# A decode block's MLP tail: w_out in longer runs, z2 before z1, three moving columns for w_out, and 1/std last

## The chip, the cores and the metric

The kernel runs on one core of a Trainium2 chip. The time is device microseconds from the first to the last instruction of that core, as a median over runs. A profile is one execution, recorded instruction by instruction. Engines are named as in the profile: PE (matmuls), PEld (their weight loads), DVE (vector), ACT (scalar), POOL (GpSimd), SP (the engine that issues nearly all transfers).

## The reference

A decode step for four sequences (B = 4, one new position each, model width D = 512), conditioned by c:

```python
mod = silu(c) @ w_mod                       # six vectors sa, ca, ga, sb, cb, gb of width 512
h = layernorm(x) * (1 + ca) + sa
x = x + ga * attention(h, k_cache, v_cache, wq, wo)   # 32 heads of 128, 4096 cached positions
h = layernorm(x) * (1 + cb) + sb
z = gelu(h @ w_in)                          # width 1792, halves z1 and z2 of 896
g = w_sp * layernorm(z2) + b_sp             # w_sp and b_sp are single numbers here (S = 1)
x = x + gb * ((z1 * g) @ w_out)
```

All inputs are bf16. The two caches hold 4 x 32 x 4096 x 128 values each, 134 MB; they make up most of the bytes.

Since the layer norm of z2 is (z2 - m) * r with one m and one r (1/std) per sequence, the last line splits: with a = (z1 * z2) @ w_out and b = z1 @ w_out, the result is gb * (w * r * a + (bs - w * r * m) * b). So w_out can be multiplied before m and r are known.

## The kernel before, in words

Everything is laid out feature-major: width 512 is four column blocks j of 128 partitions, width 896 is seven blocks jf (JF = 7), and the four sequences are the moving columns of each matmul. A vector such as modT[:, 5] (gb) is 128 partitions x 4 blocks x 4 sequences, 16 numbers per partition.

The stages are these. A preamble (lines 221 to 263) computes silu(c), LN1, the modulation (mod_part) and the queries. mod_part reads w_mod as weights: for its first two calls the 128 columns have a step of 4 elements, for the other four they are contiguous. The preamble also prepares gwb (line 258): gb times w_sp and gb times b_sp. Then a loop over 32 pairs of a head group and a sequence (lines 417 to 449) streams K and V in tiles of 4 MB and does the attention of each; two K and two V buffers alternate. SP issues the transfers in program order. In the last round it issues, after the last V pieces, the last tile of wo (line 427), the two halves of w_in (win, line 429) and the two parts of w_out (wout, line 431). The trace's names for these tiles are wo_g, win_434, win_435, wout_436 and wout_437.

The part after the loop (lines 457 to 519) is one serial tail, whose engines run their instructions in the order written:

- x1 (lines 460, 461), LN2 and h (lines 464 to 472). ln_stats forms squares, sums over the partitions with a matmul against a matrix of equal entries, reduces, and takes 1/std on ACT as Ln and then Exp.
- z (line 480): 56 matmuls. The outer loop is over the halves a of w_in. On half 0 all blocks of z2 (s = 1) and z1 (s = 0) get their first two terms, on half 1 their last two.
- gelu of z2 (line 487) and of z1 (line 491), an ACT table load back to the set that has Ln and Exp (line 492), and LN3's sums over z2 with the product z1 * z2 in between (line 494). u holds the product and z1 side by side, so that w_out has eight moving columns.
- y (line 499): 28 matmuls, first those on wout_436, then those on wout_437.
- six vector operations after Exp: gb*w*r (line 505), times m (506), gb*bs minus that (507), times y (508), the sum of the two (510), plus x1 (512). Then a transpose by matmul (514), a copy (518) and the store (519).

w_out's rows are taken as seven blocks of 128: partition p holds rows p, 128 + p, 256 + p and so on, each 1 KB long, so that one run in memory is one row.

Of the kernel before, what the change touches and what calls it, by code (L numbers as in the profile page):

```python
# [8 lines left out]
BF16 = mybir.dt.bfloat16  # L9
F32 = mybir.dt.float32  # L10
AF = mybir.ActivationFunctionType
ALU = mybir.AluOpType
# [4 lines left out]
def kernel(  # L17
# [16 lines left out]
    nc = tc.nc  # L34
    ctx.enter_context(tc.manual_schedule())
    P = 128
    B, _, D = A_x.shape
    _, H, SK, DH = A_k_cache.shape
    F = B_w_in.shape[1]
    FH = F // 2  # L40
    J = D // P
    JF = FH // P
# [12 lines left out]
    persist = ctx.enter_context(tc.tile_pool(name="persist", bufs=1))  # L55
# [40 lines left out]
    def load_k(i):  # L96
        return load(A_k_cache, i, "kt", (2, 2) if i == len(quads) - 1 else (1,))

    def load_v(i):
        return load(A_v_cache, i, "vt", (2, 4, 8, 16, 16) if i == len(quads) - 1 else (1,))  # L100
# [13 lines left out]
        out=sel, in_=ident.rearrange("p (t m) -> p m t", m=32), axis=AX.X, op=ALU.add,  # L114
# [33 lines left out]
    def bc(col, n):  # L148
        return col[:, None, :].to_broadcast([P, n, B])
# [25 lines left out]
    modT = persist.tile([P, 6, J, B], F32, name="modT")  # L175
    qbc = persist.tile([P, B, G, DH], BF16, name="qbc")
    x1b = persist.tile([P, 2, J, B], F32, name="x1b")
    wbf = persist.tile([P, 2], F32, name="wbf")
# [1 line left out]
    cT, x4T = xcT[:, :, 0:B], xcT[:, :, B:2 * B]  # L180
    xT = persist.tile([P, J, B], F32, name="xT")

    gwb = persist.tile([P, 2, J, B], F32, name="gwb")
    sT = persist.tile([P, J, B], BF16, name="sT")
    hbc = persist.tile([P, J, B, R], BF16, name="hbc")
    psum_acc = ctx.enter_context(
# [34 lines left out]
    with tc.tile_pool(name="pre", bufs=1) as pre:  # L221
        xc_ps = psum_s.tile([P, J, 2 * B], F32, name="small", bufs=1)
        for j in range(J):
            nc.tensor.matmul(
                xc_ps[:, j, :], lhsT=rows[:, j::J],
                rhs=ident[0:2 * B, 0:2 * B], start=True, stop=True,
            )
        xt_ps = psum_s.tile([P, J, B], F32, name="big", bufs=2)
        for j in range(J):
            nc.tensor.matmul(  # L230
                xt_ps[:, j, :], lhsT=rows[:, j * P:(j + 1) * P],
                rhs=ident[0:2 * B, B:2 * B], start=True, stop=True,
            )
        xb = pre.tile([P, 2, J, B], F32, name="xb")
        sg = pre.tile([P, J, B], F32, name="sg")
        nc.scalar.activation(out=sg, in_=xc_ps[:, :, 0:B], func=AF.Exp, scale=-1.0)
        nc.vector.tensor_copy(out=xcT, in_=xc_ps)
        nc.vector.tensor_copy(out=xb[:, 0], in_=x4T)
        nc.vector.tensor_scalar_add(out=sg, in0=sg, scalar1=1.0)
        nc.vector.reciprocal(out=sg, in_=sg)  # L240
        nc.vector.tensor_tensor(out=sT, in0=sg, in1=cT, op=ALU.mult)
        mean, rstd = ln_stats(pre, psum_s, xb, mean_d, J, "ln1")
        nc.vector.tensor_copy(out=xT, in_=xt_ps)
        mod_part(1)
        mod_part(0)
        hn = pre.tile([P, J, B], F32, name="hn")
        nc.vector.tensor_tensor(out=hn, in0=xb[:, 0], in1=bc(mean, J), op=ALU.subtract)
        nc.vector.tensor_tensor(out=hn, in0=hn, in1=bc(rstd, J), op=ALU.mult)
        nc.vector.tensor_tensor(out=hn, in0=hn, in1=modT[:, 1], op=ALU.mult)
        nc.vector.tensor_tensor(out=hn, in0=hn, in1=modT[:, 0], op=ALU.add)  # L250
        nc.vector.tensor_copy(out=hbc, in_=hn[:, :, :, None].to_broadcast([P, J, B, R]))
        for oc in range(2, 6):
            mod_part(oc)
        wb_ps = psum_s.tile([P, 2], F32, name="small", bufs=1)
        nc.tensor.matmul(wb_ps, lhsT=ones_b, rhs=wb_t, start=True, stop=True)
        nc.vector.tensor_copy(out=wbf, in_=wb_ps)
        for k in range(2):
            nc.vector.tensor_scalar_mul(out=gwb[:, k], in0=modT[:, 5], scalar1=wbf[:, k:k + 1])
        for b in range(B):
            for g0 in range(0, G, 4):  # L260
                qp = psum_s.tile([P, 4, DH], F32, name="big", bufs=2)
                query(b, g0, 4, qp)
                nc.scalar.copy(out=qbc[:, b, g0:g0 + 4, :], in_=qp)


    with tc.tile_pool(name="psum_att", bufs=1, space=bass.MemoryType.PSUM) as psum:
# [112 lines left out]
        def apply(i):  # L379
# [28 lines left out]

        win_v = B_w_in.rearrange("(j p) n -> p j n", p=P)
        win = [persist.tile([P, 2, F], BF16, name=f"win{a}") for a in range(2)]  # L410
        JFS = [(0, JF // 2 + 1), (JF // 2 + 1, JF)]
        wout_v = B_w_out.rearrange("(j p) n -> p j n", p=P)
        wout = [
            persist.tile([P, j1 - j0, D], BF16, name=f"wout{a}") for a, (j0, j1) in enumerate(JFS)
        ]
        st["k", 0] = load_k(0)
        for i in range(NQ):
            if i + 1 < NQ:
                st["k", i + 1] = load_k(i + 1)
            if quads[i][1] == 0:  # L420
                g = quads[i][0]
                st["wo", g] = wk.tile([P, NH, D], BF16, name="wo_g", bufs=2)
                if g < G - 1:
                    nc.sync.dma_start(out=st["wo", g], in_=wo_w[g])
            st["v", i] = load_v(i)
            if i == NQ - 1:
                nc.sync.dma_start(out=st["wo", G - 1], in_=wo_v[G - 1])
                for a in range(2):
                    nc.sync.dma_start(out=win[a], in_=win_v[:, 2 * a:2 * a + 2, :])
                for a, (j0, j1) in enumerate(JFS):  # L430
                    nc.sync.dma_start(out=wout[a], in_=wout_v[:, j0:j1, :])
            if i > 1:
                diagonal(i - 2)
            if i == NQ - 1:
                keep_busy(4)
            scores(i, 0)
            if i > 1:
                project(i - 2)
            scores(i, 1)
            if i == NQ - 1:  # L440
                softmax(i - 1)
            fold(i, 0)
            fold(i, 1)
            if i != NQ - 2:
                softmax(i)
            if i > 0:
                values(i - 1)
            if i > 1:
                apply(i - 2)
# [7 lines left out]
    with tc.tile_pool(name="post", bufs=1) as post, \  # L457
            tc.tile_pool(name="psum_post", bufs=1, space=bass.MemoryType.PSUM) as psum:
        x1 = x1b[:, 0]
# [4 lines left out]
        mean, rstd = ln_stats(post, psum_s, x1b, mean_d, J, "ln2", lambda:  # L464
            nc.vector.tensor_tensor(out=xs, in0=x1, in1=modT[:, 4], op=ALU.mult))
        nc.scalar.preload_act_table_set("gelu_apprx_tanh_and_others")
        ms = post.tile([P, J, B], F32, name="ms")
# [3 lines left out]
        h = post.tile([P, J, B], BF16, name="h")  # L471
        nc.vector.tensor_tensor(out=h, in0=xs, in1=modT[:, 3], op=ALU.add)

        zp = {s: psum.tile([P, JF, B], F32, name=f"z{s}_ps") for s in (1, 0)}
        for a in range(2):
            for s in (1, 0):
                for jf in range(JF):
                    c0 = s * FH + jf * P
                    for j in range(2):
                        nc.tensor.matmul(  # L480
                            zp[s][:, jf], lhsT=win[a][:, j, c0:c0 + P], rhs=h[:, 2 * a + j],
                            start=(a == 0 and jf == 0 and j == 0), stop=(a == 1 and j == 1),
                            skip_group_check=True,
                        )
        z2b = post.tile([P, 2, JF, B], F32, name="z2b")
        z2 = z2b[:, 0]
        nc.scalar.activation(out=z2, in_=zp[1], func=AF.Gelu_apprx_tanh)


        u = post.tile([P, JF, 2, B], BF16, name="u")  # L490
        nc.scalar.activation(out=u[:, :, 1, :], in_=zp[0], func=AF.Gelu_apprx_tanh)
        nc.scalar.preload_act_table_set("natural_log_exp_and_others")  # L492
        mean, rstd = ln_stats(post, psum_s, z2b, mean_f, JF, "ln3", lambda:
            nc.vector.tensor_tensor(out=u[:, :, 0, :], in0=u[:, :, 1, :], in1=z2, op=ALU.mult))
        y_ps = psum.tile([P, J, 2, B], F32, name="y_ps")
        for a, (j0, j1) in enumerate(JFS):
            for jf in range(j0, j1):
                for jo in range(J):
                    nc.tensor.matmul(
                        y_ps[:, jo], lhsT=wout[a][:, jf - j0, jo * P:(jo + 1) * P], rhs=u[:, jf],  # L500
                        start=(jf == 0 and jo == 0), stop=(jf == JF - 1), skip_group_check=True,
                    )

        cf = post.tile([P, J, 2, B], F32, name="cf")
        nc.vector.tensor_tensor(out=cf[:, :, 0], in0=gwb[:, 0], in1=bc(rstd, J), op=ALU.mult)
        nc.vector.tensor_tensor(out=ms, in0=cf[:, :, 0], in1=bc(mean, J), op=ALU.mult)
        nc.vector.tensor_tensor(out=cf[:, :, 1], in0=gwb[:, 1], in1=ms, op=ALU.subtract)
        nc.vector.tensor_tensor(out=cf, in0=y_ps, in1=cf, op=ALU.mult)
        q = post.tile([P, J, B], F32, name="q")
        nc.vector.tensor_tensor(out=q, in0=cf[:, :, 0], in1=cf[:, :, 1], op=ALU.add)  # L510
        yo = post.tile([P, B, J], BF16, name="yo")
        nc.vector.tensor_tensor(out=yo.rearrange("p b j -> p j b"), in0=q, in1=x1, op=ALU.add)
        t_ps = psum_s.tile([J * B, P], F32, name="small", bufs=1)
        nc.tensor.matmul(
            t_ps, lhsT=yo.rearrange("p b j -> p (b j)"), rhs=ident, start=True, stop=True,
# [34 lines left out]
```

## Time and profile before

The median of three runs is 671.23 us (671.2 to 671.52). The profiled execution took 671.3 us; its recorded span is 669.5 us.

| | busy in the span |
|---|---|
| PE | 414.7 us (62%) |
| DVE | 403.1 us (60%) |
| ACT | 41.3 us (6%) |
| POOL | 4.4 us (1%) |
| transfers | 283.17 MB at a mean of 423 GB/s |

Busy shares are averages over the whole span, and nearly all of it is the loop over K and V. The tail, which is all that the change touches, takes the last 12 us. It is read from the timeline, where each row has a start, a duration, the engine and line, the operation, the tiles (output <- inputs), the shape, and in brackets the idle time before it with what ended it. The chain of work is another view: followed back from the last instruction, it names at each step what released it. The granted clock of PE is 0.50 of full speed through the tail.

### The profile page before, as it was taken

To read this page: it belongs to the slowest core of one execution; us is meant where nothing else is said; L and a number is where in the kernel's file an instruction comes from. 1 tells how busy PE (TensorE), PEld (TensorE's weight loads), DVE (VectorE), ACT (ScalarE), POOL (GpSimd) and SP (SyncE) were. 2 spreads that over 40 slices of the span, in tenths; PEclk is the share of its full clock that TensorE was granted. 3 is DMA by queue.
4 is the path that set the end of the run, shared out by engine and by line. 5 is a ranking of instruction groups with operands and counts; after the bars stand their busy time and mean duration, and the time that the engine had idled before them with its cause. 6 is when DMAs were issued, how large, how long until landed. Compare 5 with 4: busy or idle time off the path is not lost.

```text
span 669.5 us, 6935 instructions
## 1 busy us (share of the span) xinstructions
PE 414.7 (62%) x3024; PEld 204.2 (30%) x3024; DVE 403.1 (60%) x476; ACT 41.3 (6%) x115; POOL 4.4 (1%) x20
## 2 busy tenths in 40 slices
PE   2557777655577655666655576665556655556775
PEld 2223333222233222233222333222223322223334
DVE  2166677666556676546666555756655657655752
ACT  1200000000000000000000000000000000000002
POOL 2000000000000000000000000000000000000000
PEclk9977777668887667888667888766788766788895
DMA  9999999999999999999999999999999999999995
GB/s 376 437 431 429 428 431 434 429 430 430 433 426 433 432 432 430 427 434 430 433 425 434 428 433 432 428 435 429 430 429 436 425 434 430 433 430 433 430 405 203
DMA packets 13373, 283.17 MB, mean 423 GB/s; under 512 B 1432, under 2 KB 2848, under 8 KB 4640
## 3 DMA queue, kind: packets, MB, share of 16 engines
q1 hardware_dynamic: 13264, 282.73, 98.7%
q8 instruction: 23, 0.38, 0.2%
q14 instruction: 6, 0.05, 0.0%
q0 software_dynamic: 64, 0.00, 0.0%
q10 hardware_dynamic: 16, 0.01, 0.0%
HBM read 282.73 MB, written 0.00 MB: 422 GB/s over the span
## 4 chain that ended last, share of the span: by engine, by line
DMA 61%; PE 24%; DVE 12%; ACT 1%; issue 0%; SPq 0%; DVEq 0%
DMA kt<-in_A_k_cache_dram 58%; PE s_ps L278 24%; DVE kt L273 11%; DMA wo_g<-in_A_wo_dram 3%; SPq L92 0%; PE big L338 0%; PE z_ps L480 0%; DVE S L287 0%; ACT L492 0%; ACT E L308 0%; DVE P_0_105 L311 0%; DVE P_1_109 L311 0%; PE small L155 0%; PE attn_ps L398 0%; DVE nm L305 0%
## 5 line engine op out<-in xcount | busy, mean ns | idle before, releaser
L278 PE MATMUL s_ps<-kt,ident 128*128 128x512 bf16 x1024 | 294.1, 459 | 189.0 <-DVE kt L273 189.0
L273 DVE TENSOR_TENSOR kt<-kt,qbc 128x8192 bf16<-128x8192 bf16 x64 | 282.7, 4420 | 85.9 <-DMA kt<-in_A_k_cache_dram 85.9
L278 PEld LDWEIGHTS <-ident 128*128 128x128 bf16 x1024 | 116.5, 114 | 355.3 <-issue 229.0
L287 DVE TENSOR_REDUCE S<-s_ps 128x64 f32<-128x512 f32 x64 | 44.3, 692 | 124.8 <-PE s_ps L278 124.8
L351 PE MATMUL zo_ps<-sel,osb 128*128 128x4 f32 x248 | 33.6, 259 | 25.8 <-ACT osb L344 25.8
L308 ACT ACTIVATE E<-S,nm 128x128 f32<-128x128 f32 x32 | 12.8, 401 | 567.2 <-DVE nm L305 567.2
L351 PEld LDWEIGHTS zo_ps<-sel,osb 128*128 128x128 f32 x248 | 31.1, 197 | 37.2 <-ACT osb L344 37.2
L338 PE MATMUL big<-vt,P_0_105 128*32 128x512 bf16 x352 | 21.0, 380 | 1.5 <-DMA vt<-in_A_v_cache_dram 1.5
L338 PE MATMUL big<-vt,P_2_113 128*32 128x512 bf16 x320 | 19.1, 380 | 0.0
L338 PE MATMUL big<-vt,P_1_109 128*32 128x512 bf16 x320 | 19.1, 380 | 0.0
L344 ACT COPY osb<-big 128x512 f32<-128x512 f32 x31 | 17.5, 565 | 20.1 <-PE big L338 20.1
L311 DVE TENSOR_TENSOR P_1_109<-E,mask_99 128x512 bf16<-128x512 f32 x11 | 7.6, 693 | 6.8 <-ACT E L308 6.8
L311 DVE TENSOR_TENSOR P_0_105<-E,mask_99 128x512 bf16<-128x512 f32 x11 | 7.6, 693 | 6.7 <-ACT E L308 6.7
L214 PE MATMUL big<-vt,hbc 128*32 128x512 bf16 x128 | 8.5, 430 | 5.0 <-DMA vt<-in_A_wq_dram 5.0
L338 PEld LDWEIGHTS <-P_0_105 128*32 128x32 bf16 x352 | 8.4, 96 | 9.0 <-DMA vt<-in_A_v_cache_dram 1.6
L311 DVE TENSOR_TENSOR P_2_113<-E,mask_99 128x512 bf16<-128x512 f32 x10 | 6.9, 693 | 6.2 <-ACT E L308 6.2
L372 DVE RECIPROCAL rz<-zo_ps 128x4 f32<-128x4 f32 x31 | 5.5, 176 | 8.4 <-PE zo_ps L351 8.4
L398 PE MATMUL attn_ps<-oP,wo_g 128*128 128x4 bf16 x112 | 3.8, 164 | 10.6 <-DVE oP L395 10.6
L338 PEld LDWEIGHTS <-P_1_109 128*32 128x32 bf16 x320 | 7.7, 96 | 6.7
L338 PEld LDWEIGHTS <-P_2_113 128*32 128x32 bf16 x320 | 7.6, 96 | 6.7
L398 PEld LDWEIGHTS <-wo_g 128*128 128x128 bf16 x128 | 4.3, 97 | 11.1 <-issue 10.4
L305 DVE STREAM_TRANSPOSE nm<-hb 128x32 f32<-128x32 f32 x32 | 6.8, 211 | 1.1
(218 smaller groups left out, 129.0 us busy)
## 6 DMA issues: line engine op xcount, KB each, us to landing
kt<-in_A_k_cache_dram SPq DMA_DIRECT2D x31, 4096.0 KB, 26.0
vt<-in_A_v_cache_dram SPq DMA_DIRECT2D x31, 4096.0 KB, 33.9
vt<-in_A_wq_dram SPq DMA_DIRECT2D x1, 4096.0 KB, 20.4
wo_g<-in_A_wo_dram SPq DMA_DIRECT2D x8, 512.0 KB, 26.6
kt<-in_A_k_cache_dram SPq DMA_DIRECT2D x2, 2048.0 KB, 25.6
vt<-in_w_mod_dram SPq DMA_DIRECT2D x1, 3072.0 KB, 9.9
vt<-in_A_v_cache_dram SPq DMA_DIRECT2D x1, 2048.0 KB, 18.7
vt<-in_A_v_cache_dram SPq DMA_DIRECT2D x1, 1024.0 KB, 20.8
```

The lines of the kernel that those rows point to most:

```text
L214: nc.tensor.matmul(qp[hl * R:(hl + 1) * R, 0:n], lhsT=hbc[:, j, b, :], rhs=wv[:, g0:g0 + n, hl, :], start=(j == 0), stop=(j == J - 1), til ...
L273: nc.vector.tensor_tensor(out=kt, in0=kt, in1=q[:, None, :].to_broadcast([P, HT, DH]), op=ALU.mult,)
L278: nc.tensor.matmul(ps, lhsT=ident, rhs=kt[:, :, cc * DC:(cc + 1) * DC], start=(cc == 0), stop=(cc == DH // DC - 1),)
L287: nc.vector.tensor_reduce(out=st["S", i][:, half * HT:(half + 1) * HT], in_=st.pop(("s", i, half)), axis=AX.X, op=ALU.add,)
L305: nc.vector.transpose(out=nm, in_=hb)
L308: nc.scalar.activation(out=E, in_=S, func=AF.Exp, bias=nm[:, 0:1], scale=att_scale, accum_out=rs,)
L311: nc.vector.tensor_tensor(out=P4[:, 0:NT, :], in0=E[:, :, None].to_broadcast([P, NT, NH]), in1=mask4[:, None, :].to_broadcast([P, NT, NH]) ...
L338: nc.tensor.matmul(po[32 * t:32 * t + 32], lhsT=P4[:, n0:n0 + 8, :], rhs=st["v", i][:, n0:n0 + 4, :], start=(u == 0), stop=(u == NU - 1), ...
L344: nc.scalar.copy(out=osb, in_=po)
L351: nc.tensor.matmul(st["o", i], lhsT=osb[:, n, :], rhs=sel[:, NH * n:NH * n + NH], start=(n == 0), stop=(n == 3),)
L372: nc.vector.reciprocal(out=rz, in_=st.pop(("z", i)))
L398: nc.tensor.matmul(attn_ps[:, jo, :], lhsT=wo_g[:, hl, jo * P:(jo + 1) * P], rhs=oT[:, hl, :], start=(g == 0 and hl == 0 and jo == 0), sto ...
```

## The change

Five things change in the tail, and one buffer in the preamble.

- w_out's rows are distributed differently. Of the first 512 rows, partition p holds rows 4p to 4p + 3, one run of 4 KB; of the last 384 rows it holds 3p to 3p + 2, one run of 3 KB.
- To match, the blocks of z take columns with a step: 4 for the first four blocks, 3 for the last three. These are weight loads of win with strided columns.
- The order of z is changed: for z2 first, every block with all four terms, and then the same for z1. The third matmul in order is now on the second half of w_in.
- u gets a third column group, z1 once more (the gelu writes 56 numbers per partition instead of 28), so w_out has twelve moving columns: for a, and twice for b.
- gwb becomes one tile with three groups: gb*w, a slot for -gb*w*m, and gb*bs. After the mean is known the slot is filled, gwb is multiplied by y in one operation, the third group is added to x1 on POOL (r1), the first two are added on DVE (q), q is multiplied by r, and r1 is added. Of these only the last two need Exp's result.

```diff
-    gwb = persist.tile([P, 2, J, B], F32, name="gwb")
+    gwb = persist.tile([P, J, 3, B], F32, name="gwb")
...
-        JFS = [(0, JF // 2 + 1), (JF // 2 + 1, JF)]
-        wout_v = B_w_out.rearrange("(j p) n -> p j n", p=P)
+        JFS = [(0, 4), (4, JF)]
+        wout_v = [
+            B_w_out[j0 * P:j1 * P].rearrange("(p j) n -> p j n", p=P) for j0, j1 in JFS
+        ]
...
-        for a in range(2):
-            for s in (1, 0):
-                for jf in range(JF):
-                    c0 = s * FH + jf * P
-                    for j in range(2):
+        for s in (1, 0):
+            for j0, j1 in JFS:
+                for jf in range(j0, j1):
+                    c0 = s * FH + j0 * P + jf - j0
+                    cols = slice(c0, c0 + (P - 1) * (j1 - j0) + 1, j1 - j0)
+                    for j in range(J):
                         nc.tensor.matmul(
-                            zp[s][:, jf], lhsT=win[a][:, j, c0:c0 + P], rhs=h[:, 2 * a + j],
-                            start=(a == 0 and jf == 0 and j == 0), stop=(a == 1 and j == 1),
-                            skip_group_check=True,
+                            zp[s][:, jf], lhsT=win[j // 2][:, j % 2, cols], rhs=h[:, j],
+                            start=(j == 0), stop=(j == J - 1),
                         )
...
-        u = post.tile([P, JF, 2, B], BF16, name="u")
-        nc.scalar.activation(out=u[:, :, 1, :], in_=zp[0], func=AF.Gelu_apprx_tanh)
+        u = post.tile([P, JF, 3, B], BF16, name="u")
+        nc.scalar.activation(
+            out=u[:, :, 1:3, :], in_=zp[0][:, :, None, :].to_broadcast([P, JF, 2, B]),
+            func=AF.Gelu_apprx_tanh,
+        )
...
-        y_ps = psum.tile([P, J, 2, B], F32, name="y_ps")
+        y_ps = psum.tile([P, J, 3, B], F32, name="y_ps")
...
-        cf = post.tile([P, J, 2, B], F32, name="cf")
-        nc.vector.tensor_tensor(out=cf[:, :, 0], in0=gwb[:, 0], in1=bc(rstd, J), op=ALU.mult)
-        nc.vector.tensor_tensor(out=ms, in0=cf[:, :, 0], in1=bc(mean, J), op=ALU.mult)
-        nc.vector.tensor_tensor(out=cf[:, :, 1], in0=gwb[:, 1], in1=ms, op=ALU.subtract)
-        nc.vector.tensor_tensor(out=cf, in0=y_ps, in1=cf, op=ALU.mult)
+        nc.vector.scalar_tensor_tensor(
+            out=gwb[:, :, 1], in0=gwb[:, :, 0], scalar=-1.0, in1=bc(mean, J),
+            op0=ALU.mult, op1=ALU.mult,
+        )
+        nc.vector.tensor_tensor(out=gwb, in0=y_ps, in1=gwb, op=ALU.mult)
         q = post.tile([P, J, B], F32, name="q")
-        nc.vector.tensor_tensor(out=q, in0=cf[:, :, 0], in1=cf[:, :, 1], op=ALU.add)
+        r1 = post.tile([P, J, B], F32, name="r1")
+        nc.gpsimd.tensor_tensor(out=r1, in0=gwb[:, :, 2], in1=x1, op=ALU.add)
+        nc.vector.tensor_tensor(out=q, in0=gwb[:, :, 0], in1=gwb[:, :, 1], op=ALU.add)
+        nc.vector.tensor_tensor(out=q, in0=q, in1=bc(rstd, J), op=ALU.mult)
         yo = post.tile([P, B, J], BF16, name="yo")
-        nc.vector.tensor_tensor(out=yo.rearrange("p b j -> p j b"), in0=q, in1=x1, op=ALU.add)
+        nc.vector.tensor_tensor(out=yo.rearrange("p b j -> p j b"), in0=q, in1=r1, op=ALU.add)
```

More of the change, by code (lines that the diff above doesn't have):

```diff
@@ L257 @@
         for k in range(2):
-            nc.vector.tensor_scalar_mul(out=gwb[:, k], in0=modT[:, 5], scalar1=wbf[:, k:k + 1])
+            nc.vector.tensor_scalar_mul(
+                out=gwb[:, :, 2 * k], in0=modT[:, 5], scalar1=wbf[:, k:k + 1],
+            )
         for b in range(B):
@@ L430 @@
                 for a, (j0, j1) in enumerate(JFS):
-                    nc.sync.dma_start(out=wout[a], in_=wout_v[:, j0:j1, :])
+                    nc.sync.dma_start(out=wout[a], in_=wout_v[a])
             if i > 1:
@@ L502 @@
                     )
-        cf = post.tile([P, J, 2, B], F32, name="cf")
-        nc.vector.tensor_tensor(out=cf[:, :, 0], in0=gwb[:, 0], in1=bc(rstd, J), op=ALU.mult)
-        nc.vector.tensor_tensor(out=ms, in0=cf[:, :, 0], in1=bc(mean, J), op=ALU.mult)
-        nc.vector.tensor_tensor(out=cf[:, :, 1], in0=gwb[:, 1], in1=ms, op=ALU.subtract)
-        nc.vector.tensor_tensor(out=cf, in0=y_ps, in1=cf, op=ALU.mult)
+        nc.vector.scalar_tensor_tensor(
+            out=gwb[:, :, 1], in0=gwb[:, :, 0], scalar=-1.0, in1=bc(mean, J),
+            op0=ALU.mult, op1=ALU.mult,
+        )
+        nc.vector.tensor_tensor(out=gwb, in0=y_ps, in1=gwb, op=ALU.mult)
         q = post.tile([P, J, B], F32, name="q")
-        nc.vector.tensor_tensor(out=q, in0=cf[:, :, 0], in1=cf[:, :, 1], op=ALU.add)
+        r1 = post.tile([P, J, B], F32, name="r1")
+        nc.gpsimd.tensor_tensor(out=r1, in0=gwb[:, :, 2], in1=x1, op=ALU.add)
+        nc.vector.tensor_tensor(out=q, in0=gwb[:, :, 0], in1=gwb[:, :, 1], op=ALU.add)
+        nc.vector.tensor_tensor(out=q, in0=q, in1=bc(rstd, J), op=ALU.mult)
         yo = post.tile([P, B, J], BF16, name="yo")
-        nc.vector.tensor_tensor(out=yo.rearrange("p b j -> p j b"), in0=q, in1=x1, op=ALU.add)
+        nc.vector.tensor_tensor(out=yo.rearrange("p b j -> p j b"), in0=q, in1=r1, op=ALU.add)
         t_ps = psum_s.tile([J * B, P], F32, name="small", bufs=1)
```

## The prediction

> **What bounds the kernel now.** I read the page first: the slices, the chain by line, the DMA issues. Then the chain of work in order of time for the last 15 us, the timeline of the same stretch, the instructions on w_out's second tile, and the matmuls of line 200, the only ones before the attention that load 128 weight columns with a stride. From the page:
>
> ```profile
> DMA  9999999999999999999999999999999999999995
> DMA 61%; PE 24%; DVE 12%; ACT 1%; issue 0%; SPq 0%; DVEq 0%
> ```
>
> The transfers are busy in every slice but the last; 283 MB at 423 GB/s fill the span. Nothing in the diff touches this stream before its last four issues (two halves of w_in, two of w_out). So the change can act only after the last wo tile has landed. The end of the chain, in order of time (start us, us, what):
>
> ```profile
> 634.51 23.00 DMA wo_g<-in_A_wo_dram
> ...
> 657.56 0.60 PE attn_ps L398 x16
> ...
> 660.90 0.18 DVE h L472
> 661.08 0.14 issue
> 661.22 1.78 PE z_ps L480 x56
> 663.00 0.02 issue
> 663.02 0.19 ACT u L491
> 663.21 0.02 issue
> 663.23 1.28 ACT L492
> 664.52 0.01 issue
> 664.53 0.31 ACT rstd_ln_4194 L170
> 664.83 0.02 issue
> 664.86 0.21 ACT rstd_ln_4194 L171
> 665.07 0.02 issue
> 665.10 0.19 DVE cf L505
> ```
>
> From wo's landing at 657.52 (634.51 + 23.00) the end follows in one serial chain of 12 us: attention's projection, LN2, h, the z matmuls, z1's gelu, a table load, Ln, Exp, six vector operations (L505 to L512), the last transpose, the store. w_out isn't on it. Three waits decide what the change is worth. In the timeline (start, duration):
>
> ```profile
> 661.22 0.89 PE L480 MATMUL z_ps<-h,win_434 128*128 128x4 bf16 x28 [1.75 <-DVE h L472]
> 662.08 0.91 PE L480 MATMUL z_ps<-h,win_435 128*128 128x4 bf16 x28
> 664.56 0.48 PE L499 MATMUL y_ps<-u,wout_437 128*128 128x8 bf16 x12 [0.36 <-DMA wout_437<-in_B_w_out_dram]
> ```
>
> First, the z matmuls follow each other every (0.89 - 0.166)/27 = 26.8 ns (0.166 is the length of one). The 28th starts at 661.22 + 27 x 0.0268 = 661.94; the first on win_435 should start at 661.97 and starts at 662.08. The missing 0.11 us is a wait for win_435's landing, hidden because matmul records overlap. The page shows win_434, of the same 896 KB, landing 23.5 us after its issue at 636.28, at 659.8; between 659.4 and 663.1 the DMA share is about half at some 210 GB/s, so about half of the engines still work. They owe half of win_435, 0.46 MB, and need 0.46/0.21 = 2.2 us: landing near 662.0 (an estimate), as the pause says. Second, y waits for wout_437 (0.36 us) and is done at 665.04, still 0.75 us before L508 consumes it at 665.79. Third, what L505 waits for is Exp at 665.07, behind z1's gelu and the table load.
>
> [...]
>
> ```profile
> L200 PEld LDWEIGHTS <-vt x33: 108/118/131, 10.7 to 12.2; 128*128 128x128 bf16 x33
> L200 PEld LDWEIGHTS <-vt x63: 103/104/108, 12.6 to 16.0; 128*128 128x128 bf16 x63
> ```
>
> The columns after the colon are ns, minimum/median/maximum. The first row, asked for before 12.5 us, is mod_part's first two groups, whose columns have stride 4; the second is the contiguous ones. The groups of 16 take 0.67 us against 0.57: a spacing of (0.67 - 0.173)/15 = 33.1 ns against (0.57 - 0.167)/15 = 26.9. [...] moved bytes fall from 211 to 183 GB/s between 660-661 and 662-663 us, as packets under 2 KB go from 44 to 188 (fewer engines at work may share in that). [...]
>
> **The change, part by part.**
>
> *w_out in longer runs.* 896 packets of 1 KB become 128 of 4 KB and 128 of 3 KB. The two loads now need about 664.5 - 662.0 = 2.5 us behind win. Bounds: nothing, or a tenth to a fifth of it, 0.25 to 0.5 us. They are the last issues on SP, with only the store behind them[...]. y's first wait will be u, at 664.5 below, so the end gets nothing either way. I take a landing near 664.2.
>
> *z2 whole, then z1.* The same 56 matmuls, but the third now needs win_435: two at 661.22, then PE stands until 662.08. What queues behind on PE: all of z, LN3's sums, y. The other 54 start at 662.08. Their columns have stride 4 (j of the first four) and 3 (of the last three); I take 33.1 ns for both, and 26.9 as the lower end, since stride 3 isn't in the trace. z ends at 662.08 + 53 x 0.0331 + 0.173 = 664.01 (lower end 662.08 + 53 x 0.0269 + 0.167 = 663.67), against 663.00: +1.01 us (+0.67). In the old order the win_434 half, 0.75 us, ran ahead of that landing; that is what is given up. z2 is ready at 662.08 + 25 x 0.0331 + 0.173 = 663.08, 0.45 us after the old 662.63 (662.65 less an issue gap); it isn't the last thing.
>
> *z1's gelu written twice.* 56 elements instead of 28. Rows of 16 and 28 elements take 183 ns (L236) and 0.19 us, so +0.02 us. ACT: 664.03 to 664.24, table load to 665.54, Ln to 665.86, Exp to 666.10, that is 665.07 + 1.03.
>
> *LN3's sums.* They wait on PE behind z1: 663.9 + 0.68 = 664.55, reduce 0.22, square 0.16, subtract 0.16 with gaps: var at 665.15, before the table load is done (665.54). Hidden by it.
>
> *y with three columns groups.* u's product (L494, 0.19) is ready at 664.48; 28 matmuls of 12 columns at the 29 ns of L499 ((0.61 - 0.167)/15): 664.52 + 27 x 0.029 + 0.17 = 665.47. Then gwb x y (48 instead of 32 elements, 0.21) to 665.71, and q's add to 665.92. Exp comes 0.18 us later, so it stays the gate. The mean's product (0.2) lies between var and y. All is hidden by Exp.
>
> *1/std at the end.* After Exp there were six operations: 666.48 (transpose's start) - 665.07 = 1.41 us. Now two: 0.03 + 0.19 + 0.02 + 0.20 + 0.05 = 0.49 us. Saved: 0.92 us.
>
> *r1 on POOL.* From 665.75 beside q's add and product on DVE; the yo add needs it at 666.31, so it has 0.55 us. POOL's rows here cost 0.10 (memset, one element) to 0.29 us (128x128 select)[...]. From both: 0.1 to 0.4 us, hidden. Nothing is queued behind on POOL; behind the wait on DVE is only yo.
>
> *Set-up.* gwb's two products write strided, 0.37 us at 16.85, beside DVE's 14 us wait for kt: nothing.
>
> Sum on the profile's own span: +1.01 + 0.02 - 0.92 = +0.11 us; without a stride cost -0.23. That execution took 671.3 us, the three others 671.2 to 671.52, so it is an ordinary one. Forecast 671.23 + 0.1 = 671.3.
>
> **Rivals.**
>
> A, the wait for win_435 doesn't come (it lands by 661.3). For it: no wait on win_435 is printed. Against: the 0.11 us pause. z would end at 661.22 + 55 x 0.0331 + 0.173 = 663.21; Exp at 665.30, y at about 665.0, so +0.21 + 0.02 - 0.92 = -0.69: 670.6.
>
> B, slower: r1 on POOL takes the wait. [...] L66 to L145 show POOL only in memsets, a select and DMA issues, never an add. It decides from 0.55 us on; at 1.8 us the kernel is 1.3 us slower[...]. Against: the select's first call at 2.69 us has no gap of that size before it.
>
> C, w_out is what matters: y, 0.36 us earlier. Hidden, since L508 came 0.75 us after y: 671.2, which can't be told from the forecast.
>
> D, the stream itself shifts: gwb grows from 128 to 192 bytes per partition, and tiles laid out behind it may move. DMA is 61% of the chain, so 0.3% of its pace is 1.3 us. The profile speaks neither way: 670 or 672.6.
>
> **How the numbers follow.** 0.2% is 1.34 us, about what a measurement of this kernel can tell from no change. Forecast with C: 0.78, own range 670.9 to 671.7 (both stride prices, and the 0.3 us between the runs shown). A: 0.07, B: 0.08, D: 0.07. Faster by over 0.2%: D's faster part, 0.04, as A ends within. Slower: B 0.08 and D 0.03, together 0.11. Same: 0.78 + 0.07 = 0.85. The range, 670.4 to 672.1, holds the forecast and A and leaves out B and most of D.
>
> **What would show it.** Right: two z matmuls at 661.2, a gap to 662.1, 54 more to 664.0; weight loads of about 118 ns on win; the second table load ending near 665.5; two vector operations between Exp and the transpose; r1 under 0.5 us; y starting after u, without a wait for w_out. Wrong: win matmuls that run through from 661.2 (A), a yo add that waits for POOL (B), wo's landing moved from 657.5 (D), or Exp no longer the last to come before q is scaled.

## The result, and the profile after

The changed kernel takes 668.1 us (668.07 to 668.34, six runs) against 671.22 us for the kernel before in the same comparison: a ratio of 0.9954, 95% interval 0.9941 to 0.9966. It is 3.1 us faster, and all six runs lie below all six of the kernel before (671.09 to 671.52). The prediction of 671.3 us, range 670.4 to 672.1, missed it.

The page of the changed kernel:

```profile
span 666.3 us, 6937 instructions
...
DMA packets 12734, 283.17 MB, mean 425 GB/s; under 512 B 1433, under 2 KB 1953, under 8 KB 4001
```

The same bytes moved at 425 instead of 423 GB/s. (A packet is one record of the trace's transfers. A 4 MB tile of K or V comes in packets of 32 KB, one for each partition: the trace of the kernel before has 8064 of that size, 128 for each of its 63 loads of 4 MB, 31 of K, 31 of V and one of wq.) w_out's packets are fewer, as they should be: the page counts 12734 packets in place of 13373. Where the time went is read from one kind of instruction, the vector product on a K tile that has just landed, at the same four places of the loop (the 9th, 31st, 51st and 61st of the 64 products). Timeline of the kernel before:

```profile
100.93 4.43 DVE L273 TENSOR_TENSOR kt<-kt,qbc 128x8192 bf16<-128x8192 bf16 x1
320.00 4.42 DVE L273 TENSOR_TENSOR kt<-kt,qbc 128x8192 bf16<-128x8192 bf16 x1 [3.15 <-DMA kt<-in_A_k_cache_dram]
518.03 4.43 DVE L273 TENSOR_TENSOR kt<-kt,qbc 128x8192 bf16<-128x8192 bf16 x1 [3.79 <-DMA kt<-in_A_k_cache_dram]
616.78 4.43 DVE L273 TENSOR_TENSOR kt<-kt,qbc 128x8192 bf16<-128x8192 bf16 x1 [2.98 <-DMA kt<-in_A_k_cache_dram]
```

and of the changed kernel:

```profile
100.31 4.42 DVE L276 TENSOR_TENSOR kt<-kt,qbc 128x8192 bf16<-128x8192 bf16 x1 [1.83 <-DMA kt<-in_A_k_cache_dram]
318.49 4.43 DVE L276 TENSOR_TENSOR kt<-kt,qbc 128x8192 bf16<-128x8192 bf16 x1 [1.92 <-DMA kt<-in_A_k_cache_dram]
515.81 4.43 DVE L276 TENSOR_TENSOR kt<-kt,qbc 128x8192 bf16<-128x8192 bf16 x1 [3.96 <-DMA kt<-in_A_k_cache_dram]
614.06 4.43 DVE L276 TENSOR_TENSOR kt<-kt,qbc 128x8192 bf16<-128x8192 bf16 x1 [2.88 <-DMA kt<-in_A_k_cache_dram]
```

The changed kernel is ahead by 0.62, 1.51, 2.22 and 2.72 us. From the first of these rows on the lead grows evenly, in a loop in which no instruction differs and each product takes the same 4.42 us. Before that it wanders: it is 2.25 us at the seventh product (83.68 against 81.43). e3 below, with the old placement, is 1.17 us ahead there as well, so the first 100 us don't show the effect. What ends the printed idle times is the landing of K. So the stream itself runs some 0.4 to 0.5% faster, and the lead is there before the tail begins.

The tail, which holds all the edits but gwb's tile, gained nothing. The chain of waits of the changed kernel (start us, us, what), from the landing of win's second half to the final transpose:

```profile
643.89 14.83 DMA win_435<-in_B_w_in_dram
658.72 0.04 issue
658.76 1.84 PE z_ps L487 x54
660.61 0.02 issue
660.63 0.22 ACT u L497
660.85 0.02 issue
660.87 1.28 ACT L501
...
662.49 0.21 ACT rstd_ln_4194 L171
662.70 0.02 issue
662.73 0.19 DVE q L522
...
663.01 0.20 DVE yo L524
663.21 0.04 issue
663.25 0.29 PE small L526
```

And three rows of its timeline:

```profile
654.33 0.59 PE L401 MATMUL attn_ps<-oT,wo_g 128*128 128x4 bf16 x16 [0.30 <-DMA wo_g<-in_A_wo_dram]
662.05 0.21 DVE L517 TENSOR_TENSOR gwb<-y_ps,gwb 128x48 f32<-128x48 f32 x1 [0.21 <-PE y_ps L508]
662.41 0.22 POOL L520 TENSOR_TENSOR r_4229<-gwb,x1b 128x16 f32<-128x16 f32 x1 [656.60 <-DVE gwb L517]
```

From the projection's start to the transpose's start the tail takes 663.25 - 654.33 = 8.92 us; before it took 666.48 - 657.56 = 8.92 us. The two are alike in length and differ inside: from the end of h to the end of z it is 2.75 us in place of 1.92, and from Exp's end to the transpose 0.55 in place of 1.41.

### The profile page after: what moved, and what is told of

Same layout as the page of the kernel before. It is cut to its first block, busy times and chain, and to the rows that moved or that the text cites. A ratio compares the mean times of both kernels' runs of the same rounds, so it can differ in the third digit from the quotient of the medians.

```text
span 666.3 us, 6937 instructions
## 1 busy us (share of the span) xinstructions
PE 412.9 (62%) x3023; PEld 204.2 (31%) x3024; DVE 402.9 (60%) x475; ACT 41.3 (6%) x115; POOL 4.7 (1%) x21
## 2 busy tenths in 40 slices
DMA packets 12734, 283.17 MB, mean 425 GB/s; under 512 B 1433, under 2 KB 1953, under 8 KB 4001
## 4 chain that ended last, share of the span: by engine, by line
DMA 59%; PE 25%; DVE 13%; SPq 2%; ACT 1%; issue 0%; DVEq 0%; ACTq 0%
DMA kt<-in_A_k_cache_dram 54%; PE s_ps L281 23%; DVE kt L276 11%; DMA vt<-in_A_wq_dram 3%; DMA win_435<-in_B_w_in_dram 2%; SPq L435 2%; PE big L215 1%; DVE S L290 0%; PE z_ps L487 0%; ACT E L311 0%; ACT L501 0%; DVE P_1_109 L314 0%; DVE P_0_105 L314 0%; DVE P_2_113 L314 0%; DVE nm L308 0%
```

## The experiments

**The question.** Why does a stream whose instructions the change doesn't touch run faster? The tail isn't all that the change touches: gwb grew by 64 bytes per partition (2 to 3 groups of 64), and everything allocated behind it moved by 64: hbc, win, wout, and the K, V and wo buffers. By the layout of the compiled programs the large buffers start 192 bytes past a multiple of 256 in their partition in the kernel before, and at a multiple of 256 in the changed kernel. The traces hold no addresses; that 256 is the period is shown by the runs below, the offset itself rests on the layout. Theory 1: the transfers run faster into buffers that start so. Theory 2: w_out's runs and the tail carry the gain.

**e1: only the start moved.**

```diff
     gwb = persist.tile([P, 2, J, B], F32, name="gwb")
+    pad = persist.tile([P, 16], F32, name="pad")
```

Nothing uses the tile `pad`.

> The kernel before with 64 unused bytes per partition laid out directly behind gwb, so that hbc, win, wout and the K and V buffers start where they start in the changed kernel: at a multiple of 256 bytes in a partition instead of 192 bytes past one. No instruction differs. Theory 1 (placement: the transfers run faster into buffers that start at such an address, and the tail is worth about nothing): about 668.1 us, 3.1 less than before, with the last wo tile landing near 654.3 instead of 657.5. Theory 2 (the changed w_out loads and the tail carry the gain): 671.2 us, nothing. Half and half would be 669.6.

Measured: 668.27 us against 671.42, ratio 0.9952 (0.9938 to 0.9967). The unused 64 bytes bring the whole gain. Its timeline at the last of the four tiles above:

```profile
614.06 4.42 DVE L274 TENSOR_TENSOR kt<-kt,qbc 128x8192 bf16<-128x8192 bf16 x1 [2.65 <-DMA kt<-in_A_k_cache_dram]
```

It is at 614.06, where the changed kernel is, with the old tail and w_out's old packets. What moved between 60 and 600 us, in the kernel before and then in e1:

```profile
DMA packets 8738, 232.37 MB, mean 430 GB/s; under 512 B 962, under 2 KB 962, under 8 KB 1730
```

```profile
DMA packets 8771, 233.25 MB, mean 432 GB/s; under 512 B 968, under 2 KB 968, under 8 KB 1736
```

The same stretch of time moves 0.4% more. Two rivals can be set aside. The engines that read the tiles don't work faster at the new start: the median product on K takes 4420 ns before and 4418 in e1, the median matmul on it 380 and 379. And the granted clock of PE doesn't follow the time: it is 0.771 in the profile of the kernel before and 0.771 in that of e2 below, which takes 668.4 us, and 0.774 in that of e4, which takes 671.4.

**e2: only the stream's buffers moved.** The same unused tile in a pool of its own, between the persistent tiles and the K and V buffers.

> The kernel before with the same 64 bytes between the persistent tiles and the K and V buffers, so that only kt, vt and wo_g (and the small work tiles) move; gwb, hbc, win and wout stay. Placement through the stream's own buffers: 668.0 to 668.4 us, since win and wout are 2.7 of 283 MB. If the small persistent tiles (hbc, the query and modulation vectors) matter instead: 671.2. Theory 2: 671.2.

Measured: 668.39 us, ratio 0.9956 (0.9940 to 0.9973). gwb, hbc, win and wout, which stayed, don't matter; what lies behind them does, and that is the buffers that the stream fills. (The small work tiles behind K and V moved with them. No run moves these alone, but the packet times below show that it is the transfers that get faster.)

**e3: the changed kernel, moved back.** 192 unused bytes behind its gwb.

> The changed kernel with 192 unused bytes behind gwb, so that every large buffer is again 192 bytes past a multiple of 256, as in the kernel before; the tail is as changed. Placement: 671.2 us, within 0.3 of the kernel before, since the tail's own steps come to 0.0 to 0.1. Theory 2: 668.1 us. A gain left over here is the tail's own.

Measured: 671.52 us against 671.42, ratio 1.0001 (0.9992 to 1.001). With the old start the change is worth nothing. e3's growth over the kernel before is 256 bytes in all, so a shift as such doesn't help. e1 and e3 together settle it: the start alone gives the gain, and without it nothing of the gain is left.

**e4, e5, e10: which starts are fast.** The kernel before with 128, 192 and 320 unused bytes (pad of 32, 48 and 80 elements).

> The kernel before with 128 unused bytes behind gwb: the large buffers start 64 bytes past a multiple of 256. If only a start at a multiple of 256 (or more) helps: about 671.2 us. If it is the distance to a boundary that counts and 64 is better than 192, something between 668 and 671. Theory 2: 671.2.

> The kernel before with 192 unused bytes behind gwb: the large buffers start 128 bytes past a multiple of 256. If only a multiple of 256 (or more) is fast: 671.3 us, and the common 32 KB packets keep their slower times. If 128 bytes are enough: 668.3.

> The kernel before with 320 unused bytes behind gwb: the large buffers start at a multiple of 512 bytes, where the changed kernel's start 256 bytes past one. If 256 is the boundary that counts: 668.3 us as with 64 unused bytes. If 512 would be better still: below 667.8.

| large buffers start at, past a multiple of 512 | kernel | us | ratio, interval |
|---|---|---|---|
| 192 | before | 671.42 | |
| 256 | e1 | 668.27 | 0.9952 (0.9938 to 0.9967) |
| 320 | e4 | 671.39 | 0.9999 (0.9991 to 1.0008) |
| 384 | e5 | 671.35 | 0.9999 (0.9990 to 1.0007) |
| 0 | e10 | 668.34 | 0.9950 (0.9935 to 0.9965) |

A multiple of 256 is fast, and a multiple of 512 is no better. 64, 128 and 192 past it are all equally slow. So 64 and 320 more bytes ahead of the buffers are fast, and 0, 128, 192 and (e3) 256 are not. The packets say the same: between 60 and 600 us the mean 32 KB packet took 1218.5 to 1218.6 ns in the kernel before, e3, e4 and e5, and 1214.5 in the changed kernel, e1, e2 and e10.

**e12, e13: per byte or per packet.** All 4 MB loads of K and V as two of 2 MB, once with the old start (e12) and once with 64 unused bytes (e13).

```diff
-        return load(A_k_cache, i, "kt", (2, 2) if i == len(quads) - 1 else (1,))
+        return load(A_k_cache, i, "kt", (2, 2))
-        return load(A_v_cache, i, "vt", (2, 4, 8, 16, 16) if i == len(quads) - 1 else (1,))
+        return load(A_v_cache, i, "vt", (2, 4, 8, 16, 16) if i == len(quads) - 1 else (2, 2))
```

> The kernel before with every 4 MB load of K and V issued as two of 2 MB, so that each packet is 16 KB instead of 32 KB and there are twice as many; buffers as in the kernel before, 192 bytes past a multiple of 256. If the misplaced start costs a fixed time for each packet, it costs 6.2 us instead of 3.1: about 674.5, if the split alone costs nothing. If it costs a share of the bytes: 671.4.

> The same two halves, with 64 unused bytes behind gwb, so that all large buffers start at a multiple of 256. The price of the split alone is this run against 668.27. If the cost is one per packet, the difference to the same kernel without the 64 bytes is 6.2 us; if it is a share of the bytes, 3.1.

Measured: 676.43 us with the old start, 671.28 with the fast one. The split alone costs 671.28 - 668.27 = 3.0 us. The start now costs 5.15 us (676.43 - 671.28) instead of 3.15: not twice, but far from the same. Transfers between 60 and 600 us, e12 and then e13:

```profile
DMA packets 16490, 230.68 MB, mean 427 GB/s; under 512 B 1832, under 2 KB 1832, under 8 KB 2600
```

```profile
DMA packets 16602, 232.37 MB, mean 430 GB/s; under 512 B 1841, under 2 KB 1841, under 8 KB 2609
```

In the same 540 us the fast start moves 0.7% more, against 0.4% with whole loads. The trace's records of single packets agree with a cost that doesn't grow with the packet's size: the mean 32 KB packet took 1218.5 ns in the kernel before and 1214.5 in e1, the mean 16 KB packet 616.3 in e12 and 612.2 in e13, some 4 ns more in both sizes. The quarter of the 32 KB packets that is slowest pays more (1220 ns and up against 1213). Dealt evenly to the 16 engines over which the page gives its shares, the 8064 packets of 32 KB of the kernel before are 504 for each, so 3.15 us is 6 ns a packet (an estimate), between the mean and the slow quarter. The three misplaced starts measured alike (671.39 us at 64, 671.35 at 128 and 671.42 at 192 bytes past a multiple of 256), so the cost doesn't follow the distance. In all these runs it is the start of the buffer written to that moves; what a misplaced start does inside a transfer no run shows, and e11 speaks against a price that each packet pays by itself.

**e11: K alone.** The K buffers, and wo_g and the work tiles behind them, at multiples of 256; the V buffers left.

> The kernel before with the K buffers (and wo_g behind them) at multiples of 256 bytes and the V buffers left 192 past one. If the cost is paid per packet written, whoever waits for it: half of the 3.1 us, 669.8. If only K counts, whose landing the chain waits for: 668.3. If one slow buffer spoils all: 671.4.

Measured: 669.09 us, ratio 0.9962 (0.9947 to 0.9977). Against the 671.54 of its comparison, aligning K (and wo_g) gives 2.45 us, where e10 in the same comparison gives 3.20: neither half nor all. The packet records show that half was wrong: with V still 192 bytes off, the mean 32 KB packet takes 1214.9 ns, only 0.4 more than with both aligned. 90% of these packets take at most 1213 ns, against 5% in the kernel before and 99.6% in e1; as about half of them are V's, most of V's misplaced packets ran as fast as placed ones. So a misplaced packet isn't always slow by itself; whether it takes other misplaced packets beside it, and why, is open.

**e7, e8, e9: the edits of the tail, apart.** All three have large buffers at multiples of 256; they are compared with e1's 668.27 and the changed kernel's 668.1. The kernel before measured 671.45 in their comparison, 671.42 in e1's and 671.22 in the changed kernel's, so differences of 0.2 us between these three say nothing by themselves.

e7 is the changed kernel with the old z (half by half of win, contiguous columns) and the old rows of w_out; only the end is new.

```diff
-        for s in (1, 0):
-            for j0, j1 in JFS:
...
+        for a in range(2):
+            for s in (1, 0):
+                for jf in range(JF):
+                    c0 = s * FH + jf * P
```

> The changed kernel with z in the old order on contiguous columns and with w_out's rows as before: of the change, only the third moving column, the product with 1/std at the end and r1 on POOL are left. Buffers at multiples of 256. Against the kernel before moved to such a start (668.27 us): the steps after Exp give 0.86 back (from Exp's end to the transpose 1.40 before, 0.55 in the changed kernel), less 0.02 for the longer gelu: 667.4. If w_out's old loads (landing about a microsecond after u) then become the last thing that is waited for, up to 0.4 of it is lost: 667.8. If the steps at the end are worth nothing: 668.3.

Measured: 667.84 us, the second of the expected values. Its chain says what took the rest:

```profile
650.97 10.50 DMA wout<-in_B_w_out_dram
661.47 0.05 issue
661.51 0.50 PE y_ps L505 x12
```

With two operations behind Exp instead of six, w_out's last landing is what y, and with it everything, waits for. In e9 below, whose w_out comes in long runs, the wait is gone.

e8 is e1 with only the new order of z, on contiguous columns.

```diff
+        for s in (1, 0):
+            for jf in range(JF):
+                c0 = s * FH + jf * P
+                for j in range(J):
```

> The kernel before moved to a start at a multiple of 256, with z in the new order on contiguous columns, and nothing else of the change. z's second part can no longer run before win's second half has landed: 54 matmuls after the landing instead of 28, so 26 x 27 ns = 0.70 us later than 668.27: 669.0. If the order costs nothing, as z2's sums start earlier: 668.3.

Measured: 669.01 us, 0.74 more than e1. Its timeline shows the price:

```profile
659.10 1.52 PEld L480 LDWEIGHTS <-win 128*128 128x128 bf16 x54 [0.74 <-DMA win<-in_B_w_in_dram]
659.11 1.60 PE L480 MATMUL z_ps<-h,win 128*128 128x4 bf16 x54 [0.66 <-DMA win<-in_B_w_in_dram]
```

All 54 matmuls stand behind the landing of win's second half.

e9 is the changed kernel with the old order of z on the strided columns, and w_out in long runs.

```diff
-        for s in (1, 0):
-            for j0, j1 in JFS:
-                for jf in range(j0, j1):
+        for a in range(2):
+            for s in (1, 0):
+                for j0, j1 in JFS:
+                    for jf in range(j0, j1):
...
-                    for j in range(J):
+                        for j in range(2):
```

> The changed kernel with z in the old order, half by half of win, but on the strided columns and with the long runs of w_out. The 28 matmuls behind the second half's landing take 28 x 33 ns instead of 54 x 33: 0.86 us less than the changed kernel's 668.1, that is 667.25, and 0.16 more than e7 for the strided columns unless w_out's older loads bind there. If the order was worth what it was written for (z2's sums ahead of z1): 668.1 or more.

Measured: 667.59 us (667.49 to 667.69), ratio to before 0.9943 (0.9928 to 0.9958). It is faster than both kernels, and its four runs lie below all six of the changed kernel. Its chain has no transfer behind h any more:

```profile
658.20 1.87 PE z_ps L488 x56
660.07 0.02 issue
660.09 0.22 ACT u L499
```

It gains 0.5 us on the changed kernel, or 0.7 when each is taken against its own measurement of the kernel before (671.45 - 667.59 = 3.86 us against 3.12); 0.86 was expected. The traces give 0.7: from the projection's start to the transpose's start the tail takes 662.72 - 654.54 = 8.18 us instead of 8.92. The expectation counted only what stands behind win's landing. But e9's z can't start before h, at 658.20, and its 56 matmuls in a row end at 660.07; the 54 behind the landing end at 660.61 in the changed kernel.

## Why the prediction was wrong

Its mechanism for the tail held in the main, and the tail was not what moved the time.

- *What it got right.* z: two matmuls, a stop until win's second half lands, then 54 more in 1.84 us (1.93 worked out), with weight loads of 112 to 116 ns (118). All of z costs 0.83 us more (1.01 worked out): 2.75 instead of 1.92 us from h's end. Exp's end to the transpose: 0.55 us (0.49), so 0.86 saved (0.92). r1 on POOL: 0.22 us (0.1 to 0.4), done at 662.63, before q's product starts at 662.73. y starts after u, with no wait for w_out. The second table load ends at 662.15, the sums are hidden under it. The sum was +0.11 us; the trace gives 0.00, and e3 against the kernel before 0.1. The changed kernel takes 0.2 us less than e1, but the kernel before, too, measured 0.2 us less in the changed kernel's comparison than in e1's.
- *The step that failed.* "Set-up. gwb's two products write strided [...] nothing", and behind it the opening statement that nothing in the diff touches the stream before its last four issues, so that the change can act only after wo's landing. Costing gwb I counted its instructions and not its bytes. Its growth moved the start of every buffer that the stream fills, and that is worth -3.15 us (e1), nearly thirty times the sum of the tail, over the whole loop ahead of wo's landing.
- *Rival D* named this, with gwb's 128 and 192 bytes, and got a chance of 0.07, a size of 1.3 us and no direction. It was true with 2.4 times that size, so the prediction had the cause among its rivals and priced it too low. The layout before could have been added up from the tiles' sizes, but nothing in the profile of before shows what a start is worth; packet times that spread over 1215 to 1222 ns, where the changed kernel's median is 1213, were a sign that only the comparison makes readable.
- *Rival C* (w_out's packets hidden): that they are hidden is confirmed for this change; e7 shows that they come to bind once the end is shorter. *A* and *B* did not happen: the wait on win is printed (0.57 us), and POOL's first add took 0.22 us and was done before yo could start. (A's time adds up to 671.23 - 0.69 = 670.5 us rather than 670.6; nothing hangs on it.)
- *The price of z's order* was foreseen: on contiguous columns it costs 0.74 us (e8), close to the 0.67 worked out. Not drawn from it was that the change is better without it: taking the order back in the changed kernel gives 0.5 to 0.7 us (e9), so that edit cancels what the new end gains.

## What to carry to other kernels

When a kernel lives on its transfers, an edit's effect on the layout counts with its instructions: add up the bytes ahead of the streamed buffers, and place these at a multiple of 256 bytes per partition on purpose (here worth 3.15 us for loads in packets of 32 KB and 5.15 us for packets of 16 KB). When a gain grows evenly over a loop that wasn't edited, look at what moved and not at what was rewritten; one unused tile is a cheap test, and it should be run in both directions. Keep matmuls whose operands have landed ahead of those whose operands haven't, even when another order reads more naturally: the other order cost 0.74 us here (e8), and taking it back gave 0.5 to 0.7 (e9).

## What the runs showed of the hardware

- With the stream's SBUF buffers at a multiple of 256 bytes per partition the kernel took 3.15 us of 671 less with 32 KB packets (e1) and 5.15 us of 676 less with 16 KB packets (e12, e13). Starts 64, 128 and 192 bytes past one measured alike (671.39, 671.35, 671.42 us), and a multiple of 512 brought nothing more (668.34 in e10 against 668.27 in e1). With K at a multiple of 256 and V not, most of the loss is gone too (2.45 of 3.20 us, e11).
- Splitting the 4 MB loads in two, aligned, cost 3.0 us by itself (671.28 in e13 against 668.27 in e1).
- Weight loads with strided columns, 3 and 4 elements apart, took longer than contiguous ones: 54 z matmuls take 1.84 us strided in the changed kernel and, in the same view, 1.62 contiguous in e8, some 4 ns each; the median weight load on win takes 112 to 116 ns in the changed kernel against 104 in the kernel before.
- An addition of two 128x16 f32 tiles on POOL, its first in this kernel, took 0.22 us in the changed kernel.
